# One transfer for both halves of an output store, and a new order of the same work, in a fused attention and spectral-gate kernel

## The chip, the cores and the metric

One core of a Trainium2 chip runs the whole program. The metric is the device time of one execution in microseconds; the profile is one execution taken by the hardware profiler. The engines are PE (matmul), DVE, ACT, POOL and SP; SP, POOL and ACT issue transfers, and 16 DMA engines carry them.

## The reference

Batch 8, sequence S = 3136, width D = 256, d_qk = 64, all float32:

```python
scores = (1.0 / S) * np.matmul(z, z.transpose(0, 2, 1))
x = u * np.matmul(np.maximum(scores, 0.0) ** 2, v)
proj = x @ w_proj                        # D -> 3 D
x1, x2, x3 = proj[..., :D], proj[..., D:2*D], proj[..., 2*D:]
x2_conv = irfft(rfft(x2, axis=1) * rfft(filter_fft, axis=0), axis=1)
out = (x1 * x2_conv * x3) @ w_out
```

## The kernel before

**Tiling.** The sequence is laid out as 64 x 49 (`N1`, `N2`): position n = 49 n1 + n2. A tile of 128 rows holds 64 values of n1 for two values of n2, one in rows 0 to 63 and one in rows 64 to 127. There are 25 such tiles (`NT`; the last has 64 rows), in seven chunks of columns, `CHUNKS` = 512 five times, then 256 and 320. `runs(lo, hi)` gives, for tiles lo to hi, the pieces of 64 rows: which half of the partitions (0 or 1), which tiles, and the first n2 in DRAM.

**Stages.** For each batch and chunk, PE makes scores of zT with zT (`score_mm`, two tiles at a time into a pair of PSUM banks), ACT or DVE takes the maximum with 0 into `R` (L2047, L2049) and the square into `A` (L2056, L2058; a ring of 8 buffers), and PE sums `A` against v into `ps_o` (`weigh`, `weigh_rows` by quarters of the array, L624 and L1847). Scores are symmetric: SP transposes `A` by DMA into `M1`, `M2e` or `M2o` (L1976) for the next two chunks, so an `A` buffer is free only when both the sum and the transpose have read it. `xT` (L2102) multiplies by `uT`, which SP also makes by a DMA transpose (L1647). The projections follow, then a transform along the sequence in two steps with a trip through DRAM between: `s_t` goes to `spec` (L1115), comes back as `spec_in` (L1146), is multiplied by the filter's spectrum (L1432 and on) and transformed back, `gs_t` goes to `spec` (L1480), and comes back as `conv_in` (L1175, two buffers).

**The end of a chunk (`add_end`).** PE transforms `conv_in` (`mm`), DVE multiplies by the gate into `yT` (`ev`, L1529), PE multiplies by w_out (`mo`), ACT or DVE copies to the output tile `ost` (`eo`; four tiles of 256 float32, two buffers), and `store` sends it to DRAM. Batches 0 to 5 are stored by SP; batch 6 by POOL; batch 7, the last, by POOL, ACT and SP, each piece by itself. The ends of a batch run among the next batch's attention.

**What sets the order.** A planner (`Plan`) goes through all tasks with estimated costs and emits each engine's instructions in the order in which it starts them. `ORDER` is a string with one letter for each PE task (S: scores; W and w, v: sums whole or by halves of the rows; Q: the four-quarter transforms; A, B, Z: the queues of the projections, the ends and the last ones; lower case a, b, z, x: two tasks side by side by halves), and the planner takes the first tasks of the queue that the letter names. `ENGINES` has one letter for each task that can run on ACT or DVE (a, d). A transfer has a cost on its issuing engine, a time on a shared bus (`moves`) and a delay after it (`late`). Everything that SP issues stands in one queue in this order. The tile framework adds the semaphores from the data that is read and written.

Of the kernel before, what the change touches and what calls it, by code (L numbers as in the profile page):

```python
# [33 lines left out]
LATE_OUT = 1.5  # L34
# [10 lines left out]


ORDER = (
    "ASSASSWWSSAAwwSvwSvvSwwSvvSwSvwSwSvvSBWWWWWSSSWWwwSwSwSvvSvwwvSvvSSWWAAWWWWABWBBWAAAWASSwSwwBAAvSvSw"
    "wwSSvvwvSSvSvWWBBWBWWWBAAAAWAWWSSwSWAAWAASwSwSSvvvwwwSvSvSvBWWWAWAAAWWABSwwwwSSSvvwvvwSSvwSwvSAwvSvv"
    "WAAWWWAABBWAAWAWWWSAwSwwSvSvSvSWWWWBAWAWSwSavxAAAAwSwwSwSwSvvwSvvvSvSBWAWWBWAAAWAWWSSAWAwSSwSwwSvwSv"  # L50
    "vvSwwQwSwQSvvvSvWSvQQWWWASSAWWAAAAWAWASSwwQvQwQvSwwwSSvwQvSvSvSvWWAWAWAWAAWASSwSwwSvwvSvQvwSwSwSvwvv"
    "SSvQWWWAWWAAAWAAWAQwQSwQwwQSAWAAAvvvvSSSwwwQSvSvwQSvSvWWWWAAAWWSwwwQQwQvvSQvwvQwSvQwvwSvvSSWWWWAWAAA"
    "AAAAWAAAWSwSWWQwSwSQvvSvSWAWAWWSSWAAWWAASwSwwSwwSSvvwvwvvSwSvvvSWAWBWABWAWBAWSBABWBAASwwSvSvSwSwSvSv"
    "wwSvvSwSvWAAWAWBBAWBBSSWWAAWABWBABWABwSwSwwSSvvvwSvSvwwSvvSSWAWBABAAWAAWWBAWBAWAAASwSvSwwSvvSwwSvwSv"
    "wSvwSwQvSQvvWWWWAAWBWBwSwQvSQwwwvQSvvSwSwSwwvQQvvvSvAABAAAAWBWSQSWWAABWAAWBAAWBSwQwQvSQvwSwwvSwSvQwv"
    "wvQvSSvWSSQWWWAABAAAWWWAWAAWAAwSSwQwSQvvvSSSWWWWAWSBWSwSwSwSvvwwvSwSvwvwSSvwSvvvSWWWWAAAAWAABWBSwwSv"
    "SwSwvwSvSSwvvSvSABWWBBWBAABWBWBABAAWWAAWAAAWwSSvwSvwSvSWBBBWAAABSwwSSvwSvSWWBBBBSvWWSSWWAAAAABWAAASS"
    "wwwwQvSvQvwvSSvwwQwSvvQwQvSSvWAWWBAWAWAWAABWwQwSwwSSvwvQvSwSvQvwwSvQSvvSBWAWWBWWSQQWWAAAWQwwSwSQwwSv"
    "SwvvSwSvvSvvSWAWAWWAAWBAAWAABQwwwSwSSvvvwvSQvSWAWWWSQSWWAAWSwSwwwSwwSvwSvvvvSwvwSSvvvSWBAWAAAAABAAWB"
    "AWABAWBWABSwSvwSSSwwvwSvvwSvAAABBABWBBASwvSvSSWBAWAAAWWBWBABBWBWABAAAAABSBwSwSwSvwvvSwSSwvvwSSvwwvSv"  # L60
    "vSSAAWWWWBAWAAWABABBASwwSQvBWWvSSwwSvvQwSwwSSvvQvQWWWWSWAWASwwQvQwvwSwSwSvwQSwwvvQSvvQvvSWBAWABAAWAW"
    "AWAWAQSWASwwwQQvwvSQvwwwwSvSQvvQvSvSWWWAWAAWBAWWwwSQvwvSwwSSvSvvSAWAWAWAAWAAAAWWwSSvwSSwwwSAAvSSwwwS"
    "vvvSvvvSwSvSWWABWWBAWBWABAABABSwwwSwSSvSvvSSwwwwvSvvvSSvSWBWAAAWAWWABBBABAAWAWAABAwSwSvSwwwSvwSSwvSv"
    "vwwSSvSvvvSAAWBBBWWBWWBBAWAAwSwSwSwwwSSSvvvvwwvQvSvSvwSvSAWWAAWAWAABWWAWQQwQwwSvQwwSwvwvSvQQvvSvSWAB"
    "WBBWAAWWABSSWWQSwSvwQSvwSwQvwwwvQwQvSvvvSSSWWWWAWWAAABAAWWwSQwQvwvwQwSvvSSvSWWAWWABWSQWAASwwSwwwSSAA"
    "AASvvvSwvSwvSSvvSWWWWABWWAAWABWBSwSvSwSSwwvAAWBAABAAABBBSvvSwSwwSvvSvSWAAAWBBAWAAWBWBBAWAABBWWASSwSw"
    "SvSvSwWAABWBBBSwSwSwvSSvvSvSWWWBBAWAAAWWAAAAAWAWASSwQvwSvwSwwSvvvQSwwSvvSQWWWAWSBBWABWWQwwSvvwwQvSSv"
    "wQwwwSSvvSvvQSAWAABWAAWAWWABAWSQwQvwSwSSvwwQvQvwvSQSwwwQvvSvvSWWWQSAAWAAAWABWWBAAAAWWSwQSvwSwQSvSvAB"
    "AWSWWAWABAWWSSwSwwSSvvvSwwwSvSvwvwwSvvvWWAWBWABABAAWABBBWSwSvSwASwwvSSSvvwwSvvwSwSSvvWABBAWAWAWBBABA"
    "WAWBBAABWWBSSwwwSSvSvvSWBBAAwSwSSwSvvvwSvSSWWAWWBABWWwQwSQvvSwwSwwSQvwvwSvQvwSvQvSvSWWAWWABAWWAWABSw"  # L70
    "wQSvSwwwvSSwQwvvvQSvvQQWWWBWWAWAWAwSvSwQwSwSwwSvSvvvQvwwSwSSvvvAWAAWWWBSQBWAWWBAWABWAAQwSvwSvwSQvSWZ"
    "WWWQSSWWWWBwSSvSwwSvSvWWWWWAWWWZAAAZBAZZAZBZBZBZBZZBZZZBQZBBZQQZZQZQQQBQQQQQQQBQQBZBZZZBZZZZZBZZZZZZ"
    "BZBZBZBZBBZBBBBBBBBBBBBBBBBBBBBBBB"
)

ENGINES = (
    "aaaddddaaddaaaaadaaadadaaadadaadadaaaadddaadaaaddddadadadaaadaddaadadadaaadaaaaddadaadaaaaadaaddadad"
    "aaaaadadaddaaaaddaaaaaaaaddaaaadddaddadaaaadaaaddaddaaadaaaadddadaaadadaaaddddaadaaaaadaaaaaaaddaaad"
    "dadddadaddadadadddaaddaaddadaadaaaaaadaadaadadaadaaaaaadaaadadaaaddaadaddaaaaadddadaadadaddaaaddaada"
    "adaaaaaaaaddaadadaaddaadadadaaaadaaaaadaaaaaaaaaaaadadaaaadaaaaadaadaaaaadaadaaaaddaadaaaaddaadaaaaa"  # L80
    "daadaadaadaadadadaaaadadaadadadddadddaadaadddaaaaaaaaadadaaaaaaddadaddaaadaaaddadaaaadddaadaadaaaadd"
    "dadadaaaadaddaaddadaaaaaaaaddaaaddaaaddadadaaaaadadadaadaaaadadaaddaadaaaaaaadaaaadaaadaaadaaaaaddaa"
    "aaaaaaddaaddadadadaadaaddaaaaaddaddaaaddaaaaaddaaaaddadddaddaaddaaaadaaaadadaadaddadadddaaaaaaddadaa"
    "adaddaaaaddaaaaaaaaadaddaaadaddaaaaadaadaadaaadaaaaadddaaaaaadaaaaaaadaadaadddaaaaaaaadaaaaaaaaaaada"
    "aaaaaaaaddaddaaaaaaaddadaaaaaadaaddaadaaddadaaaaaadddaadaaaddadaaadaaaadaadddaadddaaaaaaaaadaadadaaa"
    "adadaaadaddaddaaaaaaaaadaaadaadadadaaadddaaddaadaaaaaaaaadaaaadaddaaadaaadadaaaaadaadaadaaaddaaaddad"
    "aaddaaaaadaadaaddadaaaaaaaaadaaaddaaadddaaaadadadaaadddaaaddadaaadaadaddaaaadaaadaaaddadaaadddddaadd"
    "aadaddaaddadaaaaaaaadaaddadadaaaaddddddaaadadaadadaaaadaddaaaaddadaaddaaaadaadaadaaaaaaaadaaaadaaaad"
    "adaadaaaadaaaaadadaaaadddaaadaaadaaaaaadadadaaadaaadaaaaadadaaadddaaadaaaaadaadaaaaadadaaadaddaaddda"
    "dddaadaaaaaadaadaddaadaddaaaaddaaaddaaaadadaaaaaadaaddaaaaddaaaddaadaadaaaaaaaaadddaaaaaddaddaaadaaa"  # L90
    "aaadadadaaaaddadaaaaaaaadaaaaaaaddaadaaaaaaaaaaaaaaaaaaadaaaaddaaaadadadaadddadadadaaaaaddaaaaadadda"
    "adaaaaaddaddaadadaaaadaaaaaaaaaddadaadaaadddaaddaadaaaadaadaaddaaaadddaaaadaadaaaaddaddadadaaaaadada"
    "aaaaaaddadaadadaaaaaaaadadaaaaaaadaaaadadaadaddaaaadaaddaddaaaaaadaaadadaaddadadaaadddaadaaadaaaaaad"
    "aaaaaaaadaaadaaaaaaaaaadadaaaaaaaaaadaddaaaadd"
)
KINDS = {"A": "FA", "B": "FB", "Z": "FZ", "w": "W", "a": "FA", "b": "FB", "z": "FZ"}

# [397 lines left out]
def kernel(  # L495
# [12 lines left out]
    B, S, D = u.shape  # L508
# [73 lines left out]
    o_p = Pool("ost", 2, [P, 4, D], F32)  # L582
# [284 lines left out]
    for i, (t0, t1) in enumerate(zip(z_cuts, z_cuts[1:])):  # L867
        step_ = -(-(t1 - t0) // -(-(t1 - t0) // 8))
        for g0 in range(t0, t1, step_):
            nt = min(step_, t1 - g0)  # L870
# [14 lines left out]
            n = nt * dqk  # L885
# [614 lines left out]
    def add_end(b, lasts, gtasks, cs, kind="FB", src=c_p, dsts=(o_p,), late=0, behind=(), then=(), split=False, mids=(y_p,)):  # L1500
        for at, c in enumerate(cs):
# [42 lines left out]
            ob = {}  # L1544
# [43 lines left out]

            def store(i0, n, only=(0, 1), by=nc.sync, c=c, ob=ob):
                r = rows_n1(out[b])  # L1590
                for j, lo, hi, n2 in runs(T0[c] + i0, T0[c] + i0 + n):
                    if j in only:
                        by.dma_start(out=r[:, n2 : n2 + hi - lo, :], in_=ob["o"][ds(j * N1, N1), i0 : i0 + hi - lo, :])
# [602 lines left out]
```

## Time and profile before

| | us |
|---|---|
| median of 3 runs | 970.39 (969.7 to 977.35) |
| the profiled execution, its own time | 974.9 |
| its span, first to last instruction | 973.1 |

The profile shows each engine's busy time and its share of the span; the packets of each DMA queue (q1: SP's transfers, q0: POOL's, q10: ACT's) with the time that they took as a share of 16 engines; the chain of work that ended last, followed back from the last instruction; groups of equal instructions (line, engine, operation, out<-in, shape, count, then busy us and mean ns, then idle time before them and what ended it); and the transfers by line with their size. A time of landing is given for POOL's transfers alone. In 40 slices of the span the DMA engines and the bytes that they moved are:

```profile
DMA  9999899877999989997999779997999978995667
GB/s 153 172 190 150 142 178 175 175 135 174 192 211 180 148 186 209 184 151 163 198 182 189 128 141 201 201 171 134 179 175 205 214 140 171 215 194 121 190 169 233
```

The digits are tenths of the time (9 is 90% or more).

### The profile page before, as it was taken

To read this page: it belongs to the slowest core of one execution; us is meant where nothing else is said; L and a number is where in the kernel's file an instruction comes from. 1 tells how busy PE (TensorE), PEld (TensorE's weight loads), DVE (VectorE), ACT (ScalarE), POOL (GpSimd) and SP (SyncE) were. 2 spreads that over 40 slices of the span, in tenths; PEclk is the share of its full clock that TensorE was granted. 3 is DMA by queue.
4 is the path that set the end of the run, shared out by engine and by line. 5 is a ranking of instruction groups with operands and counts; after the bars stand their busy time and mean duration, and the time that the engine had idled before them with its cause. 6 is when DMAs were issued, how large, how long until landed. Compare 5 with 4: busy or idle time off the path is not lost.

```text
span 973.1 us, 26702 instructions
## 1 busy us (share of the span) xinstructions
PE 933.5 (96%) x10403; PEld 516.1 (53%) x10403; DVE 856.1 (88%) x1484; ACT 843.3 (87%) x1169; POOL 197.4 (20%) x426
## 2 busy tenths in 40 slices
PE   7999999999999999899998999998999999999895
PEld 3444555465555655465544665555555565556554
DVE  8888799989999988898887998896999999899785
ACT  7976899998799989899887999888988989998573
POOL 5222212220302211122111221222012220101031
PEclk9999999999999999999999999998999999999988
DMA  9999899877999989997999779997999978995667
GB/s 153 172 190 150 142 178 175 175 135 174 192 211 180 148 186 209 184 151 163 198 182 189 128 141 201 201 171 134 179 175 205 214 140 171 215 194 121 190 169 233
DMA packets 332430, 170.76 MB, mean 175 GB/s; under 512 B 242598, under 2 KB 307942, under 8 KB 332304
## 3 DMA queue, kind: packets, MB, share of 16 engines
q1 hardware_dynamic: 302424, 132.28, 67.7%
q0 software_dynamic: 29168, 35.13, 25.4%
q8 instruction: 81, 1.33, 0.6%
q10 hardware_dynamic: 712, 1.66, 0.6%
q14 instruction: 45, 0.37, 0.1%
HBM read 90.26 MB, written 53.35 MB: 148 GB/s over the span
## 4 chain that ended last, share of the span: by engine, by line
PE 79%; DMA 10%; DVE 4%; ACT 3%; issue 2%; SPq 2%; DVEq 0%; POOL 0%; ACTq 0%; POOLq 0%
PE ps_s L624 32%; PE ps_o_t L1847 29%; PE ps_o_t L624 17%; DMA M2e_t<-A_t 2%; DMA M_t<-A_t 1%; DMA spec<-s_t 1%; DMA M_t<-spec_in_t 1%; DMA M2o_t<-A_t 1%; ACT R_t L2047 1%; ACT A_t L2056 1%; DMA A_t<-spec 1%; DMA spec<-gs_t 1%; DVE R_t L2049 1%; DVE xT_t L2102 1%; DMA conv_in_t<-spec 1%
## 5 line engine op out<-in xcount | busy, mean ns | idle before, releaser
L2047 ACT ACTIVATE R_t<-ps_s 128x1024 f32<-128x1024 f32 (+4 forms) x347 | 322.8, 966 | 31.1 <-PE ps_s L624 22.6
L1847 PE MATMUL ps_o_t<-A_t,v_t 64*64 64x512 bf16 (+3 forms) x3852 | 319.8, 355 | 0.1
L2056 ACT ACTIVATE A_t<-R_t 128x1024 bf16<-128x1024 f32 (+2 forms) x311 | 300.9, 995 | 20.0 <-DMA M2o_t<-A_t 7.2
L1847 PEld LDWEIGHTS <-v_t 64*64 64x64 bf16 (+1 forms) x5296 | 185.5, 103 | 153.4 <-PE ps_o_t L1847 32.2
L2058 DVE TENSOR_TENSOR A_t<-R_t 128x1024 bf16<-128x1024 f32 (+4 forms) x181 | 201.1, 1126 | 20.9 <-ACT R_t L2047 11.8
L2049 DVE TENSOR_SCALAR R_t<-ps_s 128x1024 f32<-128x1024 f32 (+2 forms) x165 | 183.0, 1120 | 25.3 <-PE ps_s L624 15.1
L624 PE MATMUL ps_s<-zT_t 64*64 64x512 bf16 (+5 forms) x1558 | 185.8, 352 | 12.6 <-ACT gs_t L699 3.8
L624 PE MATMUL ps_o_t<-A_t,v_t 128*128 128x512 bf16 (+2 forms) x760 | 178.3, 354 | 0.1
L749 POOL COPY tick<-xT_t 1x1 bf16<-1x1 bf16 x54 | 10.3, 190 | 661.9 <-DVE xT_t L2102 661.9
L624 PEld LDWEIGHTS <-v_t 128*128 128x128 bf16 x1046 | 95.0, 98 | 84.8 <-issue 23.3
L624 PE MATMUL ps_s<-xT_t,wp 128*128 128x512 bf16 (+2 forms) x434 | 110.5, 353 | 0.3 <-DVE yT_t L1529 0.3
L699 ACT ACTIVATE x_t<-ps_s 128x512 bf16<-128x512 f32 (+2 forms) x155 | 84.2, 577 | 29.8 <-PE ps_s L624 25.4
L624 PEld LDWEIGHTS <-zT_t 64*64 64x64 bf16 (+1 forms) x1591 | 66.3, 102 | 73.0 <-issue 31.7
L1432 DVE TENSOR_TENSOR xh<-xh,H 128x1024 bf16<-128x1024 bf16 x120 | 81.8, 685 | 7.4 <-ACT xh L699 6.0
L2102 DVE SCALAR_TENSOR_TENSOR xT_t<-ps_o_t,uT_t 128x256 bf16<-128x256 f32 (+2 forms) x224 | 75.2, 381 | 12.1 <-issue 6.2
L1330 DVE TENSOR_TENSOR gate_t<-ps_s,x_t 128x256 bf16<-128x256 f32 (+2 forms) x216 | 72.7, 383 | 9.0 <-PE ps_s L624 5.1
L1847 PE MATMUL ps_o_t<-M_t,v_t 64*64 64x512 bf16 (+3 forms) x912 | 75.3, 363 | 0.8 <-DMA M_t<-spec_in_t 0.8
L1529 DVE TENSOR_TENSOR yT_t<-ps_s,gate_t 128x512 bf16<-128x512 f32 (+2 forms) x99 | 59.8, 621 | 11.2 <-PE ps_s L624 9.5
L740 POOL DMA_DIRECT2D un_t<-in_u_dram x112 | 60.0, 557 | 7.7 <-issue 4.0
L759 POOL DMA_DIRECT2D v_t<-in_v_dram x112 | 59.3, 551 | 6.9 <-issue 4.1
L699 ACT ACTIVATE s_t<-ps_s 128x512 bf16<-128x512 f32 (+1 forms) x86 | 50.1, 593 | 11.9 <-PE ps_s L624 11.5
L624 PEld LDWEIGHTS <-wp 128*128 128x128 bf16 x448 | 42.1, 98 | 33.6 <-issue 4.5
(177 smaller groups left out, 1030.7 us busy)
## 6 DMA issues: line engine op xcount, KB each, us to landing
out_dram<-ost_t SPq DMA_DIRECT2D x60, 256.0 KB
spec<-s_t SPq DMA_DIRECT2D x96, 128.0 KB
spec_in_t<-spec SPq DMA_DIRECT2D x56, 192.0 KB
spec<-gs_t SPq DMA_DIRECT2D x56, 192.0 KB
v_t<-in_v_dram POOLq DMA_DIRECT2D x80, 128.0 KB, 5.3
un_t<-in_u_dram POOLq DMA_DIRECT2D x80, 128.0 KB, 6.3
conv_in_t<-spec SPq DMA_DIRECT2D x34, 256.0 KB
out_dram<-ost_t SPq DMA_DIRECT2D x18, 128.0 KB
```

What stands on the lines that cost most here:

```text
L624: inst = nc.tensor.matmul(o, *args, **kw)
L699: got = nc.scalar.activation(out_, in_, AF.Copy)
L740: nc.gpsimd.dma_start(out=t[ds(j * N1, N1), lo - t0 : hi - t0, :], in_=x[:, n2 : n2 + hi - lo, :])
L1330: got = nc.vector.tensor_tensor(g[:, ::-1] if h == 0 else g, p, x, ALU.mult)
L1432: nc.vector.tensor_tensor(x[:, 1 - i], x[:, 0], h, ALU.mult)
L1529: got = nc.vector.tensor_tensor(yb["y"][:, dh, 0:w], p, gates[b, c, dh][:, 0:w], ALU.mult)
L1847: row_sums[dh] = h, nc.tensor.matmul(*args, **kw)
L2047: has_read(nc.scalar.activation(r, p, AF.Relu), p)
L2049: has_read(nc.vector.tensor_single_scalar(r, p, 0.0, ALU.max), p)
L2056: nc.scalar.activation(a, r, AF.Square)
L2058: (nc.vector if e == "DVE" else nc.gpsimd).tensor_tensor(a, r, r, ALU.mult)
L2102: nc.vector.scalar_tensor_tensor(x, f, inv_s2, ut, ALU.mult, ALU.mult)
```

## The change

`store` gets a second way. Where the two pieces of a store (rows 0 to 63 and 64 to 127) have the same tiles, one transfer is issued with both: its output side has an outermost step of two pieces, then 64 rows, then the contiguous columns; its tile side is the 128 rows. That holds for the chunks 0 to 5 of the batches 0 to 6 (36 stores on SP, 6 on POOL). The last chunk, whose last tile has 64 rows, and batch 7, whose pieces go to different queues, are stored as before. The planner's cost of such a store on SP falls from 1.3 to 0.85. Both strings are replaced; what each task computes stays.

```diff
 ORDER = (
-    "ASSASSWWSSAAwwSvwSvvSwwSvvSwSvwSwSvvSBWWWWWSSSWWwwSwSwSvvSvwwvSvvSSWWAAWWWWABWBBWAAAWASSwSwwBAAvSvSw"
+    "ASSASSSWWAAwSwSvSvwSvwwSvSwvSSvwwSvvSSWWWWWSSWBWwwSwwSvvwwSSvvSvSvSWAAWWWWWABWBBWAAWAAwSwSwwSBWASvv"
...
 ENGINES = (
-    "aaaddddaaddaaaaadaaadadaaadadaadadaaaadddaadaaaddddadadadaaadaddaadadadaaadaaaaddadaadaaaaadaaddadad"
+    "aaaddddaaddaaaddaaaaaadaaadadaadadaddddddaadaaaddddadadadaaadaddaaddadaddadaaadadaaaadaddaddaaaadaaa"
...
             def store(i0, n, only=(0, 1), by=nc.sync, c=c, ob=ob):
                 r = rows_n1(out[b])
-                for j, lo, hi, n2 in runs(T0[c] + i0, T0[c] + i0 + n):
+                got = runs(T0[c] + i0, T0[c] + i0 + n)
+                if only == (0, 1) and len(got) == 2 and got[0][1:3] == got[1][1:3]:
+                    (_, lo, hi, n2), (_, _, _, m2) = got
+                    o = r[:, n2 : n2 + hi - lo, :]
+                    o = bass.AP(o.tensor, o.offset, [[(m2 - n2) * D, 2], list(o.ap)[0], [1, (hi - lo) * D]])
+                    by.dma_start(out=o, in_=ob["o"][:, i0 : i0 + hi - lo, :].rearrange("p t d -> p (t d)"))
+                    return
+                for j, lo, hi, n2 in got:
                     if j in only:
                         by.dma_start(out=r[:, n2 : n2 + hi - lo, :], in_=ob["o"][ds(j * N1, N1), i0 : i0 + hi - lo, :])
...
-                s_ = on("SP", lambda nt=nt, store=store: store(0, nt), 1.3, [*oe, *behind], prio=1, moves=0.45 * nt, late=LATE_OUT * (dst is o_p))
+                s_ = on("SP", lambda nt=nt, store=store: store(0, nt), 0.85 if c < NC - 1 else 1.3, [*oe, *behind], prio=1, moves=0.45 * nt, late=LATE_OUT * (dst is o_p))
```

How SP's queue stands at the first store of batch 0, among the attention of batch 1: the store, then transposes of scores (`M_t`, `M2e_t`) and of u (`uT_t`); a row is a line, the transfer and the shape of its output. Before:

```order
L1175 DMA conv_in_t<-spec_0_61 128x4x256
L1115 DMA spec_1_60<-s_t 128x2x256
L1593 DMA out_dram<-ost_t 64x1024 x2
L1976 DMA_TRANSPOSE M_t<-A_t 128x8x128
L1647 DMA_TRANSPOSE uT_t<-un_t 128x8x128
L1976 DMA_TRANSPOSE M_t<-A_t 128x8x128
L1976 DMA_TRANSPOSE M2e_t<-A_t 128x8x128 x2
```

and now:

```order
L1115 DMA spec_1_60<-s_t 128x2x256
L1175 DMA conv_in_t<-spec_0_61 128x4x256
L1596 DMA out_dram<-ost_t 2x64x1024
L1983 DMA_TRANSPOSE M_t<-A_t 128x8x128
L1654 DMA_TRANSPOSE uT_t<-un_t 128x8x128
L1983 DMA_TRANSPOSE M_t<-A_t 128x8x128
L1983 DMA_TRANSPOSE M2e_t<-A_t 128x8x128 x2
```

The two stores of 64 rows have become one of 2 x 64 rows; four transposes stand behind it as before.

Later in the same batch, SP's queue from a pair of transposes on: the stores of further chunks, the load of the last end chunk (`conv_in_t`) and the first loads of batch 1's spectrum (`spec_in_t`). Before:

```order
L1976 DMA_TRANSPOSE M_t<-A_t 128x8x128 x2
L1702 DMA_TRANSPOSE zT_t<-zd_t 128x8x128
L1647 DMA_TRANSPOSE uT_t<-un_t 128x8x128
L1976 DMA_TRANSPOSE M2o_t<-A_t 128x8x128 x2
L1593 DMA out_dram<-ost_t 64x1024 x2
L1175 DMA conv_in_t<-spec_0_61 128x3x256
L1146 DMA spec_in_t<-spec_1_60 48x2048 x2
```

and now:

```order
L1654 DMA_TRANSPOSE uT_t<-un_t 128x8x128
L1983 DMA_TRANSPOSE M2o_t<-A_t 128x8x128
L1115 DMA spec_1_60<-s_t 128x2x256
L1596 DMA out_dram<-ost_t 2x64x1024 x2
L1175 DMA conv_in_t<-spec_0_61 128x3x256
L1115 DMA spec_0_59<-s_t 128x2x256
L1146 DMA spec_in_t<-spec_1_60 48x2048 x2
```

One more whole store has moved here, so that two merged stores follow each other, with the `conv_in` and spectrum loads behind them.

Near the start, DVE's queue where the first scores are squared (`A_t<-R_t`) and `xT` of chunk 0 is made. Before:

```order
L2049 TENSOR_SCALAR R_t<-ps_s_140 128x1024
L2058 TENSOR_TENSOR A_t<-R_t 128x1024 x2
L703 COPY T_220<-ps_s_139 128x128
L703 COPY T_220<-ps_s_139 128x64
L2058 TENSOR_TENSOR A_t<-R_t 128x1024
L2102 SCALAR_TENSOR_TENSOR xT_t<-ps_o_t,uT_t 128x4x64 x4
```

and now:

```order
L2056 TENSOR_SCALAR R_t<-ps_s_141 128x1024
L2065 TENSOR_TENSOR A_t<-R_t 128x1024 x3
L2109 SCALAR_TENSOR_TENSOR xT_t<-ps_o_t,uT_t 128x4x64 x4
L2065 TENSOR_TENSOR A_t<-R_t 128x1024
L703 COPY T_220<-ps_s_139 128x128
L703 COPY T_220<-ps_s_139 128x64
```

The copies of the transform's table have gone behind `xT`, and a square has moved ahead of it. Over the whole program the order moves nine of the 128x1024 squares from ACT (247 to 238) to DVE (141 to 150) and adds 158 rows on PE (20,806 to 20,964), where more sums run by quarters.

More of the change, by code (lines that the diff above doesn't have):

```diff
@@ L47 @@
 ORDER = (
-    "ASSASSWWSSAAwwSvwSvvSwwSvvSwSvwSwSvvSBWWWWWSSSWWwwSwSwSvvSvwwvSvvSSWWAAWWWWABWBBWAAAWASSwSwwBAAvSvSw"
[L49 to L72, printed above, removed]
@@ L73 @@
-    "BZBZBZBZBBZBBBBBBBBBBBBBBBBBBBBBBB"
+    "ASSASSSWWAAwSwSvSvwSvwwSvSwvSSvwwSvvSSWWWWWSSWBWwwSwwSvvwwSSvvSvSvSWAAWWWWWABWBBAWAAWAAwSwSwwSBWASvv"
+    "SwSwSSvvvSvSWWWWBBWWBAAWABWWAAwSSSwWAAAWBAvSwSvwwwSSvSvSvvSAWWWBWAAAWWwSSwSWAWAvwvSwSwSvwvvwSSvSvWWA"
+    "WAWAABBAWWWWWAwSSwwSvSvSvSAAWWWWBAAWWSwSavxSwBAAAwSwSvvwSvwSwSvSvvWBWAWAAWAAWWASSAWAWWSSSwwwSvSvQwwS"
+    "wQwvSSvvwSvvQvWQSWAAWWSSAAWWAAAWWASwwQvQvQSwwwSQvSvSwvSvwSSvWWWAWAAWAAAWSSSwwwwSvQvSwSwvSvwSvwvvSSvQ"
+    "WWWAWWAWAAAWAAQQwSwwQwSQvWAAAAvvvSSwSvwwQwSQvSvvSSAWWWWAAWWQwwSvQvQwwQSvwQvwSvQvwwSSvvSWWAAAWWWAAAAA"
@@ new lines @@
+    "WAAAWwSSWWQSSwwQvvvSSWAAAWWWSSSWAAWAWAwSwwSSwwSvvvvwSwwSvSvvwvSvAWBWAWBAWWABBWAABBSwwSvSwvSSvwSvwSwS"
+    "vvSwSvWAWAABBBWASSAWABWWBABWBWAWwSwSwSwSvvSwvwvSwvSSvSvWAWABWAAAWBBBWAABAAAAAWWSwSwSSwwSvvwwSvvSwSvS"
+    "vwvSvwQvQWWBWWABAWWSwSwQwQvwQwSvwvSSvvwQvwQwSvSvvBAAAABWWSQSWWAABWBWAAAAWAABSwQvQSwwwSwwSQSvwwvvQSvQ"
+    "vSvvSWWWWSQAWAAWAWAWBAWAAAASwSQwwQSvvSvSSWWWWAWSSBWWSSwwSvvwwSwSSvvwwwvSSvvSvWWWAAWAWAAABWBwSwSwSwwS"
+    "vvvSSvwSvSvSWWBBABABWBWAAABBWAWBWAAABAWBWASwSwSvvwSABABSwwvSvwwvSSvwSvSBBWBBWSSvSWBBAWAAWAWAAAAAWSSw"
@@ new lines @@
+    "wQSwwSvQvvSwvwwwQSwQvvvSQvvSWAWAAWAWWBAWWwSwQwSwwQSvvvSSQvwQwwvSvSvSvBWAWABWWQQSWWABWAAwwwQSSwwwQSvv"
+    "vSwvwSSvvSvvSWBWWWAAAAWAAAWSwQvwwSSvwSvwQvvSWWWWQSSWWAAAWAwwSwSSwwwwSvSvvSvvwvvSvwSSvWWAWWBAABAAAABA"
+    "WABAABWABASwSwSSwSvwwwvvSSvwSvvBAAABBvSwwSBBWBASvvSAWBWBAWABBABBWAAWAABAAABWSwSwwASvvSSwwSvSwvwwSvSS"
+    "vvvSWWWWBAWAABAWABBAwQSwBAWWSSSvwwwwvQwSSvvSvvvQQSWWWSWAWAWQwwSvwQwvwSSQvwwSSvvwwQvSvvQSvWWABBWWAAWA"
+    "AWAAwQwQwAWASvQwSvvSQwwvwSQvSvvQwSSvWWWWABWAWAAwSwwQSvwwwvvSvSvvSSWWAAAWAAWAWAAAWwSSvSwSwwwSAASSvwwS"
@@ new lines @@
+    "wvvwSvSSvvvvSWAWWBWBWABWABAABABwSSwwwSSSvwvSvSwwwvSvvSSvvSWWABAAWBBAABAWWAAWBABAAAWwSwSSvwwwSSvSvSvw"
+    "vwwwSSvvvvSSWBAWABBBWBWWBAAAAAWSwSwwwSSvvSvwSvwSwwwQvvSvvSvSWAAWWWAABAWAWWQQwQwwSQvwwSwwQvvSvSvQvvSW"
+    "BAWABAWWWBBSSWWSQwSvwwSwQSvwQwvSwwQvQvvvvSwSSvWWWBWAAWAAAAWWSQwwQvwwQwvSvvSSvSWAWAWAWAWBWSwSSwSwwwQv"
+    "SAAAASwwSvSvwvvvSvSvSWWBWWAAAWABABWWASSwSvwSSwvwwBBBWAABBASvvSvwwSvSwvSSvSWBWWBAABBWAWAABAABAAAAWWSS"
+    "wSvwwSSvWAABABBWABBSSvwSSwwSvSvvSWWABBWWAWAAAWAAWAAASwwwSQvSvwvSwSwwwSQvvSvvSvWWQSWWAWABWWBWBAQwSvww"
@@ new lines @@
+    "SQvwvwQSwSQvvvSwSSvWAAWWABWAABWAAWSQwSvwQvwwSQSvwvwQvSwwvQwSQvvvSSWWWWQSAWAWwAAAABWAWBAAAQvwSwSwSvSQ"
+    "vSvSAWAWBWWAWABAWwSSvwSwwwvSSvSwwwvwvSSSvvvvWWWBABAWAAWABABWSwwSSvWBBAAwSwSSvvvSwSvwSwSvvSWBBWWBBWWA"
+    "BWBAAABAABABWAWSSwwwSSSvvwvSBBAAwwSvSSvvSwSSvWWWWBAWSAWBWSQwwwSvSwwvvQSvvQwwQSvwvSwSSvvQWWAAWWAABWWA"
+    "BWwSwSQvwSvwwQSwvSvvwQQvvQSWWWWWAAWBAWwSwQvSvSwSwSvvwwSQvvwwSwSSvvvWABWBAWWAWQSWAWAWAWZBAAQwSwSwQvSS"
+    "vvBWWWBWQSSWWwwSSvwvSwwSvvvSWAWWWWWWWAZZAZAZAZAZBBBZZBBZZBZZZBQZBZZQQZBQQBQQQQQQQZQQBQQBZZZBZZBZZZZZ"
@@ L74 @@
+    "ZZZZZBZBBZBZBZBBZBBBBBBBBBBBBBBBBBBBBBBB"
 )
 ENGINES = (
-    "aaaddddaaddaaaaadaaadadaaadadaadadaaaadddaadaaaddddadadadaaadaddaadadadaaadaaaaddadaadaaaaadaaddadad"
[L78 to L91, printed above, removed]
@@ L92 @@
-    "adaaaaaddaddaadadaaaadaaaaaaaaaddadaadaaadddaaddaadaaaadaadaaddaaaadddaaaadaadaaaaddaddadadaaaaadada"
-    "aaaaaaddadaadadaaaaaaaadadaaaaaaadaaaadadaadaddaaaadaaddaddaaaaaadaaadadaaddadadaaadddaadaaadaaaaaad"
-    "aaaaaaaadaaadaaaaaaaaaadadaaaaaaaaaadaddaaaadd"
+    "aaaddddaaddaaaddaaaaaadaaadadaadadaddddddaadaaaddddadadadaaadaddaaddadaddadaaadadaaaadaddaddaaaadaaa"
+    "adaaadadaddaaaaaddaadaaaaddaadaaddaaaadadddaaadaadaddaadadadadaaddaadaddadaadaadaaddaaaaadadaadaadad"
+    "dadaaddadaddadadddaaddaaddadaadaaaadadaadaaadadaaadaadadaaadadaaaddaadaddaaaaaddaadaaaadaddaaaadddaa"
@@ new lines @@
+    "adaaaaaaaaadaadadaaddaadadadaaaaadaaaaddadaaaaaaaaadadddaadaaaaadaadaaaaadaaaadaaddaaaaaaaddadaaaaaa"
+    "dddadaadddadaaaaadddadadaaaddadddadddaddaaaddaaaaaaaaadadaaaaaadaaaaddaaadaadadadaaaadddaadaaaadddad"
+    "daaaadadaaaddaaaaddaaaaaadaaadaaddaaaddadadaaadaaadadaaaaaaadadaaadaadaaaaaaaddaaadaaadaaadadddaddaa"
+    "aadaaadaaaddadaddaaaaaaddaadaaaaaaaaaddaaadadaddaaaadaaaaaddadaaaddadaaaaaaaadadddadadadaaaaaaddadaa"
+    "adaadaadddaddaaadaaaddddadaaaddaaaadaaadaadaaadaaaaadddaddadaaaaaaaaaaaaadaaddadaaaaadaaaaadaaaaaada"
@@ new lines @@
+    "aaaaaadaddaddaadaadaddaaaaddaaaaaaddaadaddddadddaadaaaadadaddaaddaaaadaddaddddaadaaddadadaaaaadadaaa"
+    "adadaaadaddaddaaaaadadaadaaaaaaddadadaaddaaadadaaaadaaddadaaaaaadadaaaaaadadaaaaadaadaadaaaaaaaaddad"
+    "aadaaadaadaadaaaaadaaaaaaaadaddadaaadadaddaddadadaaadddaaadaddddadaadadadaaadaaadaaaddddaaaadaadaaaa"
+    "aaaaddaaddadaaaaaaaadaaddadadaaaaadaaadaddaddaadadaaaddadddadaaaadadaaaaaaaddaadaaaaaadaaddaaaaaaaad"
+    "adaaadadaaaaaaadadaaaadddaaaaadaaaaaaaadaaadaaaaaaaaaaddadadaaadddaaaddaadadaadaadaadadaaadaddaaddda"
@@ L95 @@
+    "dddaadadddaadaaadaaaadaddadaaddaaaddaadadadaddaadaaadaaadaadaaadadadaadadaaadaaadddaaadaadaddaaadaaa"
+    "aaadadadaaaadaaddaaaaadadaaaaaaaddaadaaaaaaaaaaaaaaaaaaadadaaadaaaaadaaaaaddadaaadaaaaaaddaaaaaaddad"
+    "aadaaddaaaaadadadaaaadaadaaddaaaadaaaadaaadaaddaddaaaadddaaadadaaaadddaaaadaadaaaaaaaddadaddaaaadada"
+    "aaaaaadaaddaaaaddaddaaadadaaaaaaddaaaadadaadadaaaaaaaaddadaadaaaadaaadadaaddadadaadddaaaaaaaaaaaaaad"
+    "aaaaaaaadaaadaaaaaaaaaadadaaaaaaaaaadadaddaadd"
 )
```

## The prediction

> **What bounds the kernel now.** I read the page first (busy time, chain of waits, DMA queues and issues), then the DMA view and the busy time by stretch of the window in which one batch is stored, then the long chain and the waits for the transfers in it. The page:
>
> ```profile
> span 973.1 us, 26702 instructions
> PE 933.5 (96%) x10403; PEld 516.1 (53%) x10403; DVE 856.1 (88%) x1484; ACT 843.3 (87%) x1169; POOL 197.4 (20%) x426
> q1 hardware_dynamic: 302424, 132.28, 67.7%
> q0 software_dynamic: 29168, 35.13, 25.4%
> PE 79%; DMA 10%; DVE 4%; ACT 3%; issue 2%; SPq 2%; DVEq 0%; POOL 0%; ACTq 0%; POOLq 0%
> ```
>
> PE is busy in 96% of the span and makes 79% of the chain that ends last. But the packets of the two large queues (SP's transfers on q1, POOL's on q0) fill 67.7 + 25.4 = 93% of the 16 DMA engines' time, and the chain runs through DMA for 10%, some 97 us. So this kernel has two resources near their end, and the second one is what the change touches. The span of the profiled execution is 973.1 us and its own time 974.9; the median of the shown runs is 970.4, so I make the sum as a difference to 974.9 and set it on 970.4.
>
> Where DMA stands in the chain (start, length, transfer):
>
> ```profile
> 399.90 7.64 DMA spec<-s_t
> 503.60 8.47 DMA M_t<-A_t
> 515.24 9.10 DMA M2e_t<-A_t
> 648.31 10.46 DMA M2o_t<-A_t
> ```
>
> and SP's own line of time around the second of them (start, time in the queue, line):
>
> ```profile
> 497.92 2.10 SPq L1593 DMA_DIRECT2D out_dram<-ost_t  x2
> 500.29 3.22 SPq L1976 DMA_TRANSPOSE M2e_t<-A_t  x1
> 503.60 6.68 SPq L1976 DMA_TRANSPOSE M_t<-A_t  x2
> ```
>
> A transpose of scores that SP issues soon after a pair of stores lands 8.5 us after its issue and something waits for its end. There is no slack to speak of behind a store, even today. The waits say the same: squares stand still until a transpose has given their A buffer back.
>
> ```profile
> ACT A_t L2056 <- DMA M2o_t<-A_t: 7.2, 3, 5.4
> ACT A_t L2056 <- DMA M2e_t<-A_t: 6.0, 2, 5.0
> DVE A_t L2058 <- DMA M2e_t<-A_t: 5.4, 2, 3.5
> ```
>
> **The change, part by part.**
>
> *Fewer issues.* On SP 36 pairs of stores become 36 single ones (30 of 512 KB, 6 of 256 KB), on POOL 6 pairs do (5 and 1).
>
> ```profile
> out_dram<-ost_t SPq DMA_DIRECT2D x60, 256.0 KB
> out_dram<-ost_t SPq DMA_DIRECT2D x18, 128.0 KB
> 350.65 1.69 SPq L1593 DMA_DIRECT2D out_dram<-ost_t  x2
> 354.41 1.28 SPq L1593 DMA_DIRECT2D out_dram<-ost_t  x2
> 364.86 1.18 SPq L1593 DMA_DIRECT2D out_dram<-ost_t  x2
> 378.25 1.16 SPq L1593 DMA_DIRECT2D out_dram<-ost_t  x2
> 398.59 1.21 SPq L1593 DMA_DIRECT2D out_dram<-ost_t  x2
> 417.62 1.18 SPq L1593 DMA_DIRECT2D out_dram<-ost_t  x2
> ```
>
> (The 18 of 128 KB are 12 of the pairs' halves and 6 of the last tile rows, which stay apart.) A pair takes about 1.18 us of SP's queue, so one issue less is 0.59 us, 36 x 0.59 = 21 us of SP in all. SP's queue is 2% of the chain, so I give this 0, and at most 2% of 21, under 1 us.
>
> *The new strings.* The same arithmetic in another order. On DVE nine squares of 128x1024 more, on ACT nine less, and some more evictions go the same way:
>
> ```profile
> L2056 ACT ACTIVATE A_t<-R_t 128x1024 bf16<-128x1024 f32 x247 | 257.8, 1067 | 16.5 <-DMA M2o_t<-A_t 7.2 <-DMA M2e_t<-A_t 6.0 <-DVE R_t L2049 1.6
> L2058 DVE TENSOR_TENSOR A_t<-R_t 128x1024 bf16<-128x1024 f32 x141 | 169.9, 1219 | 16.0 <-ACT R_t L2047 7.2 <-DMA M2e_t<-A_t 5.4 <-ACT s_t L699 2.2
> ```
>
> That is 9 x 1.07 = 10 us off ACT and 9 x 1.22 = 11 us onto DVE, both of which stay under PE's 933.5. PE's 158 added rows are the same sums cut into quarters. What an order can win is PE's idle time, 973.1 - 933.5 = 39.6 us, of which the first and the last microseconds stay; what it can lose has the same size. I take -3 us, with -10 and +10 as ends.
>
> *The shape of the transfer.* This is the term that decides. Before, each piece is 64 rows of 4 KB, out and in. Now the output side is counted as 2 pieces, 64 rows, 4 KB, outermost first, and the tile's side as 128 rows, 1, 4 KB. On how many of the 16 engines does that lie? The trace shows how transfers are divided. In the last 12 us ACT's queue (q10) carries five stores of 64 rows and nothing else; in the 19 us from 921 it carries four loads of nine rows and nothing else:
>
> ```profile
> gs_t<-spec ACTq DMA_DIRECT2D x4, 36.0 KB
> q10 hardware_dynamic: 400, 1.11, 28.8%
> q10 hardware_dynamic: 72, 0.15, 3.7%
> ```
>
> (window 962 to 974, then 921 to 940; packets, MB, share of 16 engines). 400 packets are 5 x 64 rows and 80 more, 16 for each store. 72 are 4 x 9 rows and 36 more, 9 for each load. So a transfer ends with one small packet on each engine that took part: 16 with 64 rows, 9 with 9. It is divided by its outermost count. No transfer in this trace has different outermost counts on its two sides. With 2 on one side and 128 on the other I take 2: every row shown is divided by whole steps of the outer count, and two steps give two engines.
>
> The Trainium skill says so outright: by its page "DMA: Bandwidth & Descriptors", section "Why a DMA increments its semaphore by 16 and not by 1", the number of engines is the largest up to 16 that divides the slowest count of both sides, and they are the lowest-numbered ones; for 2 and 128 that is 2. The trace agrees for 64 and for 9 rows, and cannot show 2 against 128.
>
> Price of a store on two engines. The same row of q10 gives a row's time: 28.8% of 16 engines x 12 us = 55.3 us for 1.11 MB, so 0.20 us for 4 KB and 0.10 us for 2 KB. Today a pair puts 8 rows on each engine, 1.6 us (0.8 us for 2 KB rows). On two engines it puts 64 rows on each, 13.0 us (6.5 us): 11.4 us more on those two (5.7 us), and nothing on the other 14. Everything SP issues behind it has a sixteenth of its bytes on these two and ends when that part ends.
>
> What of it reaches the end? Take one batch's stores, all six between 350 and 430 (rows above). The stretch (length, busy PE, PEld, DVE, ACT, POOL, clock, DMA share, GB/s):
>
> ```profile
> 350.00:430.00 80.00, 76.69 (x869) 41.07 (x868) 71.42 (x124) 69.61 (x94) 15.24 (x32) 1.00 1.07 186
> ```
>
> - Upper end: the share is true occupation. The two engines carry 1.07 x 80 = 85.6 us now, less today's stores 5 x 1.6 + 0.8 = 8.8, plus the new 5 x 13.0 + 6.5 = 71.5: 148 us of work in 80 us, 68 us too much. Over the whole span the share is 93%, so next to nothing is worked off in the rest of the batch: +68 us a batch.
> - Lower end: a share above one shows that packets overlap on an engine, so it overstates the need. The most that the trace shows is the 436 GB/s in this row (GB/s in 40 slices of 955 to 972), 27 GB/s an engine, 4 KB in 0.15 us.
>
> ```profile
> GB/s 153 181 318 252 370 354 365 380 383 436 387 390 366 270 135 87 29 0 0 260 193 164 241 328 222 301 297 183 241 193 183 366 260 318 376 390 285 236 72 0
> ```
>
> By bytes the stretch needs 186/436 x 80 = 34 us, less 6.6 of today's stores, plus 5 x 9.6 + 4.8 = 52.8: 80 us in 80. Then nothing is left over: +0 a batch.
>
> Between 0 and 68 I take the middle, 34 us: the small packets of the transposes do not run at the peak rate, and the chain's rows of 8 to 10 us behind stores show that lateness is paid at once; but PE's waiting thins the other traffic out, which works against the upper end. SP stores six batches (batches 0 to 5): 6 x 34 = 204 us, ends 0 and 408. Behind such a store SP's queue holds the transposes, uT, the conv_in loads of the next end chunk and the spec loads (the order rows above), and for these wait, in turn, the squares (A buffers), PE's mirrored sums, DVE's xT, and PE's end chunks. The A ring's eight buffers and the two of conv_in and ost cover part of 11.4 us; when that cover is gone the rest is PE's.
>
> *POOL's six stores.* These rows carry the price now (last number: us to landing):
>
> ```profile
> out_dram<-ost_t POOLq DMA_DIRECT2D x8, 256.0 KB, 3.4
> out_dram<-v_t POOLq DMA_DIRECT2D x2, 256.0 KB, 4.6
> ```
>
> They have few followers, in the last batch. On 16 engines they cost 0; on two, at most one more batch's 34 us. I take 0 and keep 34 for the range.
>
> Sum: 974.9 + 0 - 3 + 204 + 0 = 1175.9 for an execution like the profiled one; on the median, 970.4 + 201 = 1171. I say 1175.
>
> **Rivals.**
>
> *Sixteen engines after all* (the other side): the transfer is divided by its 128 rows of the tile. Then each engine has the same 8 rows, 1.6 us, and only the 21 us of SP and the new order are left: 970.4 - 3 = 967, between 958 and 985. For it: the tile's side is as good a count as the other, and the trace does not show which one rules. Against it: the count of end packets follows the outermost step. It decides from the point where the split gives 16 parts; below that the rows per engine rise. The same skill page, in "Rules for kernel authors", speaks for the change: two transfers to disjoint partition halves share the same engines anyway, use one of 128 partitions. Here that would give these 967; but the rule below it, on using all 16 engines, wants the large count outermost, and this transfer has 2 there.
>
> *Two engines, but absorbed*: the rings of A, M and conv_in take the lateness, and only one store a batch is paid in full, 6 x 11.4 = 68 us: 970.4 + 68 = 1038, from 985 to 1060. For it: the lower end above. Against it: the waits for A buffers today.
>
> *The two engines become the bound throughout*: the share is true occupation, 970.4 + 408 - 3 = 1375, from 1320 on. For it: a DMA share of 1.07 in the stretch. Against it: a share over one cannot be occupation.
>
> **How the numbers follow.** Forecast (two engines, half of the excess paid, 1060 to 1320) 0.67; sixteen engines 0.15; absorbed 0.10; bound throughout 0.08. Two engines in any form are 0.85. The range reaches from 990 to 1340: it holds the forecast (0.67), nearly all of the absorbed case (0.09) and the lower half of the last (0.04), 0.80 together; the sixteen-engine case lies outside. One per cent (9.7 us; the three runs before spread by 0.8%) is about what a measurement of this kernel can tell from no change. Slower by more: 0.85 and the slow tail of the sixteen-engine case (worse strings), 0.03, together 0.88. Within: 0.08 of that case. Faster by more: its remaining 0.04.
>
> **What would show it.** Two engines: SP's queue q1 loses 36 x (160 - 130) = 1080 packets (a pair has 128 rows and 32 end packets, the merged store 128 and 2); sixteen: 36 x 16 = 576. The DMA share of a stretch of stores falls well under one while transposes behind a store take over 12 us in the chain, and DMA's part of the chain rises from 10% to 20% or more. ACT and DVE wait longer for A buffers, PE idles some 200 us more, nearly all of it before 845, in the batches that SP stores. The forecast is wrong if q1 loses about 576, or if it loses 1080 and the chain still has DMA at about 10%.

## The result, and the profile after

| | before | changed |
|---|---|---|
| median, us | 973.87 (969.7 to 991.12, 4 runs) | 1217.9 (1216.08 to 1228.77, 4 runs) |
| ratio, 95% interval | | 1.2547 [1.2432, 1.2662] |
| profiled execution, own time / span, us | 974.9 / 973.1 | 1216.08 / 1214.3 |

The change costs a quarter of the time. The ratios here and below leave out executions more than 1.5% above the fastest of the same kernel (here 991.12), so a ratio can differ a little from that of the medians. The page of the changed kernel (busy times; the queues' packets, MB and share of 16 engines; the chain by engine; the stores):

```profile
span 1214.3 us, 26789 instructions
PE 994.4 (82%) x10482; PEld 541.8 (45%) x10482; DVE 873.2 (72%) x1505; ACT 839.7 (69%) x1148; POOL 194.9 (16%) x420
q1 hardware_dynamic: 301344, 132.27, 65.0%
q0 software_dynamic: 34000, 35.15, 20.0%
PE 51%; DMA 31%; DVE 5%; ACT 4%; issue 4%; SPq 3%; another core or an unknown queue 0%; ACTq 0%; DVEq 0%
out_dram<-ost_t SPq DMA_DIRECT2D x30, 512.0 KB
out_dram<-ost_t POOLq DMA_DIRECT2D x4, 512.0 KB, 18.6
```

Three things are to be read. SP's queue carries as many bytes as before (132.28 and 132.27 MB) in 302424 - 301344 = 1080 packets fewer, which is 36 x 30 to the packet: each merged store ends on 2 engines (2 end packets in place of 32). DMA's part of the chain rises from 10% to 31%. And no engine has become busier by much (PE the most, from 933.5 to 994.4 us, of which more at the end); PE goes from 96% to 82% of a longer span.

The two engines can be seen at work. The DMA view of the changed kernel from 400 to 412 us, in 40 slices (share in tenths of 16 engines, then GB/s):

```profile
DMA  9768997798998532111101111186211110111110
GB/s 191 120 150 178 198 203 155 126 154 135 176 154 161 130 82 68 48 34 41 36 19 32 22 32 29 26 251 169 60 43 44 63 55 41 55 55 55 55 55 41
```

From the middle on the share is one tenth, with a burst between, and at the end 55 GB/s in slice after slice: two engines of 16 are an eighth of the share, and 55 / 2 = 27.5 GB/s each is 4 KB in 0.149 us. From 409.2 to 413 us SP's queue is alone, and its packets take 13.0% of 16 engines, 2.1 engines:

```profile
q1 hardware_dynamic: 70, 0.20, 13.0%
```

The other 14 stand idle while a 512 KB store runs out. SP's line of time there (start, time in the queue, line):

```profile
396.52 5.90 SPq L1596 DMA_DIRECT2D out_dram<-ost_t  x1
402.52 4.77 SPq L1115 DMA_DIRECT2D spec<-s_t  x1
...
413.47 0.52 SPq L1596 DMA_DIRECT2D out_dram<-ost_t  x1
414.09 3.29 SPq L1115 DMA_DIRECT2D spec<-s_t  x1
417.48 10.13 SPq L1983 DMA_TRANSPOSE M_t<-A_t  x1
```

Even the issue is held back: a transpose that takes 1.2 to 1.3 us of SP's queue where nothing holds it, and took 3.2 to 3.3 us behind a pair of stores in the prediction's rows, takes 10.13 us behind the merged store. In the chain (start, length) this transpose and others now stand with 11.7 to 16.7 us, beside stores and a load that a later step waits for:

```profile
236.56 12.11 DMA M_t<-A_t
391.82 14.67 DMA out_dram<-ost_t
417.48 16.66 DMA M_t<-A_t
479.10 11.70 DMA M_t<-A_t
559.32 15.99 DMA out_dram<-ost_t
744.21 14.96 DMA spec_in_t<-spec
```

Who pays (waiting engine, what for, us in total, times, longest):

```profile
ACT A_t L2063 <- DMA M_t<-A_t: 59.7, 14, 13.4
DVE A_t L2065 <- DMA M_t<-A_t: 42.6, 6, 13.2
ACT ost_t L699 <- DMA out_dram<-ost_t: 39.4, 6, 8.8
```

The squares wait for `A` buffers, 102 us in these two rows, and evictions wait for `ost` tiles. By the Trainium skill (page "DMA: Bandwidth & Descriptors", section "Why a DMA increments its semaphore by 16 and not by 1") such a transfer lies on 2 engines; the trace agrees, with 1080 packets fewer and 55 GB/s.

### The profile page after: what moved, and what is told of

Same layout as the page of the kernel before. It is cut to its first block, busy times and chain, and to the rows that moved or that the text cites. A ratio compares the mean times of both kernels' runs of the same rounds, so it can differ in the third digit from the quotient of the medians.

```text
span 1214.3 us, 26789 instructions
## 1 busy us (share of the span) xinstructions
PE 994.4 (82%) x10482; PEld 541.8 (45%) x10482; DVE 873.2 (72%) x1505; ACT 839.7 (69%) x1148; POOL 194.9 (16%) x420
## 3 DMA queue, kind: packets, MB, share of 16 engines
q1 hardware_dynamic: 301344, 132.27, 65.0%
## 4 chain that ended last, share of the span: by engine, by line
PE 51%; DMA 31%; DVE 5%; ACT 4%; issue 4%; SPq 3%; another core or an unknown queue 0%; ACTq 0%; DVEq 0%
PE ps_o_t L1854 21%; PE ps_s L624 20%; DMA M_t<-A_t 11%; PE ps_o_t L624 10%; DMA out_dram<-ost_t 6%; DMA spec_in_t<-spec 3%; DMA conv_in_t<-spec 2%; DMA M2e_t<-A_t 2%; DMA A_t<-spec 2%; DMA spec<-M2o_t 1%; DVE R_t L2056 1%; DMA spec<-s_t 1%; ACT R_t L2054 1%; DVE A_t L2065 1%; DMA M_t<-spec_in_t 1%
## 5 line engine op out<-in xcount | busy, mean ns | idle before, releaser
L2054 ACT ACTIVATE R_t<-ps_s 128x1024 f32<-128x1024 f32 (+3 forms) x349 | 325.3, 964 | 76.4 <-PE ps_s L624 34.4
L1854 PE MATMUL ps_o_t<-A_t,v_t 64*64 64x512 bf16 (+4 forms) x3886 | 337.8, 369 | 14.6 <-issue 9.8
L1854 PEld LDWEIGHTS <-v_t 64*64 64x64 bf16 (+1 forms) x5390 | 201.2, 107 | 188.1 <-issue 45.2
L2065 DVE TENSOR_TENSOR A_t<-R_t 128x1024 bf16<-128x1024 f32 (+3 forms) x191 | 211.7, 1126 | 96.5 <-DMA M_t<-A_t 42.6
L624 PE MATMUL ps_s<-zT_t 64*64 64x512 bf16 (+5 forms) x1570 | 196.7, 366 | 54.7 <-ACT ost_t L699 24.0
L2056 DVE TENSOR_SCALAR R_t<-ps_s 128x1024 f32<-128x1024 f32 (+4 forms) x163 | 180.0, 1118 | 58.8 <-PE ps_s L624 39.3
L2109 DVE SCALAR_TENSOR_TENSOR xT_t<-ps_o_t,uT_t 128x256 bf16<-128x256 f32 (+2 forms) x224 | 75.3, 383 | 23.3 <-PE ps_o_t L624 12.1
L624 PE MATMUL ps_s<-wo,yT_t 128*128 128x256 bf16 (+1 forms) x344 | 56.7, 289 | 16.3 <-DVE R_t L2056 10.7
L699 ACT ACTIVATE ost_t<-ps_s 128x512 f32<-128x512 f32 (+1 forms) x57 | 33.4, 590 | 52.0 <-DMA out_dram<-ost_t 39.4
L699 ACT ACTIVATE xh<-ps_s 128x512 bf16<-128x512 f32 (+1 forms) x71 | 41.5, 611 | 33.4 <-PE ps_s L624 33.1
L624 PE MATMUL ps_s<-wp,xT_t 128*128 128x256 bf16 (+1 forms) x408 | 61.4, 278 | 3.3 <-ACT ost_t L699 2.5
```

The costliest lines, as they stand in the source:

```text
L624: inst = nc.tensor.matmul(o, *args, **kw)
L699: got = nc.scalar.activation(out_, in_, AF.Copy)
L1854: row_sums[dh] = h, nc.tensor.matmul(*args, **kw)
L2054: has_read(nc.scalar.activation(r, p, AF.Relu), p)
L2056: has_read(nc.vector.tensor_single_scalar(r, p, 0.0, ALU.max), p)
L2065: (nc.vector if e == "DVE" else nc.gpsimd).tensor_tensor(a, r, r, ALU.mult)
```

## The experiments

The theory is "two engines": the count of outermost steps on the output side sets how many engines a store lies on, and its rows there delay all the rest. Its rivals: "strings" (the new order costs), "one transfer" (the length of a merged store costs, wherever it lies), the shape by itself, and the place in SP's queue. Ratios are to the kernel before on the same chip.

**The new order without the merged stores.**

```diff
-                if only == (0, 1) and len(got) == 2 and got[0][1:3] == got[1][1:3]:
+                if False and len(got) == 2 and got[0][1:3] == got[1][1:3]:
```

> The changed kernel with every store again as two transfers of 64 rows; the new strings and the planner's cost stay, so PE, DVE and ACT stand in the changed kernel's order. Theory 'two engines' (a store whose output side has 2 outermost steps lies on 2 of the 16 DMA engines, and all that SP issues behind it waits there): the loss is gone, 960 to 985 us, q1 at 302424 packets again, DMA about 10% of the chain. Theory 'strings' (the new order of the tasks costs the time): 1190 to 1230 us.

Measured: 968.22 us against 978.23, ratio 0.9914 [0.9872, 0.9955], q1 302424. The loss is gone, with DMA at 11% of the chain; the order by itself gains 0.9%, and this kernel beats both others. Its busy times and its chain:

```profile
PE 927.8 (96%) x10403; PEld 520.2 (54%) x10482; DVE 867.1 (90%) x1505; ACT 834.0 (86%) x1148; POOL 196.4 (20%) x426
PE 75%; DMA 11%; DVE 6%; ACT 3%; issue 3%; SPq 1%; ACTq 0%; DVEq 0%
```

**The merged stores in the old order.** The kernel before with the new `store` and nothing else of the diff.

> The kernel before, with its own strings and costs, and the merged store on SP and POOL. 'Two engines': nearly all of the loss, 1180 to 1240 us, q1 at 301344 packets (1080 fewer). 'Strings': 965 to 985 us. If strings and stores each had a share, the two kernels of this comparison would both lie between.

Measured: 1.266 [1.2588, 1.2732], 1236.11 us, q1 301344. The whole loss, and a little more, is the stores'.

**Only SP's, and only POOL's.** The same kernel with one more condition in `store`:

```diff
-                if only == (0, 1) and len(got) == 2 and got[0][1:3] == got[1][1:3]:
+                if by is nc.sync and only == (0, 1) and len(got) == 2 and got[0][1:3] == got[1][1:3]:
```

(`nc.gpsimd` for POOL's.)

> The kernel before with SP's 36 stores merged and POOL's as they were: the main term by itself. With POOL's stores at 1.024 and all merged at 1.266, additive costs give 1.24, some 1205 to 1220 us; if POOL's and SP's stores hinder each other, less than 1.23.

> The kernel before, with only POOL's six stores of batch 6 merged. The prediction took 0 for them, at most 34 us. 'Two engines' on POOL's queue as well: landing of the 512 KB stores some 13 us or more in place of 3.4, time 970 to 1005 us; if POOL's transfers lie on 16 engines whatever their shape: landing of 4 to 6 us, 968 to 978 us.

Measured: SP's alone 1.2502 [1.2383, 1.2621], 1215.7 us against 972.03; POOL's alone 1.0243 [1.019, 1.0297]. Together 25.0 + 2.4 = 27.4%, with 26.6% measured: they add up within their intervals. POOL's stores, with POOL's alone merged:

```profile
q0 software_dynamic: 34000, 35.15, 24.7%
out_dram<-ost_t POOLq DMA_DIRECT2D x4, 512.0 KB, 16.0
out_dram<-v_t POOLq DMA_DIRECT2D x1, 512.0 KB, 23.9
out_dram<-v_t POOLq DMA_DIRECT2D x1, 256.0 KB, 21.1
```

Landing takes 16 to 24 us where 256 KB took 3.4 to 4.6. The end packets cannot tell the engines here, because this queue's count rises (see the end), but its share can. In this kernel's trace POOL's queue is alone from 943.5 to 945.9 us, behind the first merged store, and again from 949 to 952, with four issued:

```profile
q0 software_dynamic: 53, 0.07, 12.0%
q0 software_dynamic: 77, 0.24, 36.3%
```

12.0% of 16 engines is 1.9, and 36.3% is 5.8. That fits two engines for each store here too, other ones for the next store, and three stores at work in the second window. And they do have followers. The chain of this kernel in the last batch:

```profile
957.74 13.39 DMA spec<-M2o_t
971.61 14.22 DMA A_t<-spec
```

The last batch's writes of its spectrum, which POOL and SP issue behind these stores, and the loads of the end chunks take 13.4 and 14.2 us there. That they wait for the engines of these stores is read from the order and the times. In the same places of its chain the kernel before had:

```profile
944.09 3.16 DMA spec<-uT_t
951.33 7.66 DMA A_t<-spec
```

That is 27.6 us in place of 10.8.

**The count of outermost steps by itself.** The kernel before, with SP's stores as 72 transfers of 64 rows, each written as g steps of 64 / g rows; the rows are taken in strides so that the steps stay apart, and they land in another order in the output. The two lines of the edit that make the shape, with g for the number in them:

```diff
+                            row = list(o.ap)[0][0]
+                            o = bass.AP(o.tensor, o.offset, [[row, g], [g * row, N1 // g], [1, (hi - lo) * D]])
```

> The kernel before; each of SP's 72 stores of 64 rows stays a transfer of its own, but its output side is counted as 2 steps of 32 rows (every second row), so the rows inside a piece of 64 land in another order in the output. 'Two engines': as slow as the merged store, 1180 to 1260 us, q1 at 302424 - 72 x 14 = 301416 packets. Theory 'one transfer' (it costs that both halves go in one long transfer, on however many engines): 965 to 985 us, since each half is again by itself.

> As pairs_outer2, with 4 outermost steps of 16 rows in each of SP's 72 stores (the rows inside a piece land in another order). 'Two engines' in its general form (as many engines as outermost steps): 16 rows of 4 KB on each of four engines for each piece, so half the excess on each loaded engine: 24 rows a pair more than on sixteen in place of 56; between 1020 and 1110 us, q1 at 302424 - 72 x 12 = 301560 packets. If only the shape's being three steps costs (longer work in making the transfer), as slow as with 2: 1250 to 1270 us.

> As pairs_outer2, with 8 outermost steps of 8 rows. General 'engines as outermost steps': 8 rows of 4 KB a pair more on each of eight engines, 970 to 1000 us, q1 at 302424 - 72 x 8 = 301848. Shape alone: 1250 to 1270 us.

> As pairs_outer2, with 16 outermost steps of 4 rows: the control. The form of the transfer is the same three-step one, but it lies on all 16 engines: 965 to 985 us, q1 at 302424. Shape alone: 1250 to 1270 us.

The last column divides the loss by the rows of 4 KB that a loaded engine has more than before (a 256 KB pair counts as half): 33 x (128 / g - 8).

| g | q1 packets | ratio, 95% | loss, us | rows more | us a row |
|---|---|---|---|---|---|
| 2 | 301416 | 1.2949 [1.2856, 1.3042] | 288 | 1848 | 0.156 |
| 4 | 301560 | 1.1136 [1.0952, 1.1319] | 111 | 792 | 0.140 |
| 8 | 301848 | 1.0352 [1.0198, 1.0506] | 34 | 264 | 0.130 |
| 16 | 302424 | 0.9967 [0.9895, 1.0038] | none | 0 | |

All four packet counts are as expected. The time follows the number of engines and goes to nothing at 16, so neither "one transfer" nor the shape stands: these are again 72 transfers, of the same three-step form in all four. The expected times for 2 engines (1180 to 1260) and 8 (970 to 1000) were a little low, by 3 and 11 us.

The page of g = 8, where each loaded engine has only 8 rows a pair more, shows that there is no slack even for that: DMA is at 16% of the chain.

```profile
PE 70%; DMA 16%; DVE 5%; ACT 4%; issue 2%; SPq 2%; ACTq 0%; DVEq 0%
```

**By another queue.** The merged stores of SP issued by ACT.

```diff
-                    by.dma_start(out=o, in_=ob["o"][:, i0 : i0 + hi - lo, :].rearrange("p t d -> p (t d)"))
+                    (nc.scalar if by is nc.sync else by).dma_start(out=o, in_=ob["o"][:, i0 : i0 + hi - lo, :].rearrange("p t d -> p (t d)"))
```

> The kernel before, SP's 36 stores merged and issued by ACT's queue in place of SP's, at the same place of the program; POOL's stores as before. If what costs is the order in the queue (SP's transposes and loads stand behind 64 rows on two engines of their own queue): 1000 to 1110 us, since another queue's rows share those engines by turns. If it is the two engines' time (64 rows of 4 KB on each, whoever issues them): 1180 to 1250 us. q1 at 302424 - 5760 = 296664 packets either way, ACT's queue at 712 + 36 x 130 = 5392.

Measured: 1.242 [1.2256, 1.2584], 1212.61 us, with the packets moved as expected:

```profile
q1 hardware_dynamic: 296664, 114.97, 72.6%
q10 hardware_dynamic: 5392, 18.96, 4.2%
```

The place in SP's queue is not what costs: out of it the loss is the same within the intervals, and an issue takes ACT's queue only 0.52 to 1.12 us. It is the two engines' time, whoever issues.

**Half of the stores.** Merged for chunks 0, 2 and 4 alone.

```diff
-                if by is nc.sync and only == (0, 1) and len(got) == 2 and got[0][1:3] == got[1][1:3]:
+                if by is nc.sync and c in (0, 2, 4) and only == (0, 1) and len(got) == 2 and got[0][1:3] == got[1][1:3]:
```

> As sp_merged_alone, but only the stores of chunks 0, 2 and 4 are merged: 18 stores of 512 KB of 30 (and none of the six of 256 KB). If each merged store's excess on its two engines enters in full, 18 / 33 of the loss (a store of 256 KB counts as half): 0.55 x 235 = 128 us, 1090 to 1120 us. If the buffers cover a part that is exceeded only when stores follow each other closely, less: 1000 to 1070 us.

Measured: 1.1338 [1.1212, 1.1465], 1105.26 us. 13.4 of 25.0% is 0.53 of the loss for 18 / 33 = 0.55 of the rows: the loss grows in step with the stores, and the buffers cover no more of it when the stores stand further apart. It is 130 us for 18 x 56 = 1008 rows, 0.129 us a row.

No run has a third `ost` tile, so what the wait for tiles is worth by itself stays open.

## Why the prediction was right

**Mechanism.** Right at the step that decided: from the end packets of ACT's queue (16 for 64 rows, 9 for 9) the prediction took the division by outermost steps, so 2 engines for the merged store, and gave 1080 packets as the sign. It is 1080. That the side with 2 steps rules, and not the one with 128, no trace before could show; it was a choice, put down as one, and the runs with g steps against 64 rows bear it out. The rival with 16 engines, 967 us, falls; its price was nearly that of the new order alone, 968.22. The absorbed rival, 985 to 1060, falls with the measured time.

**The main term** was 204 us, 34 a batch; SP's stores alone measured 0.2502 x 972.03 = 243 us, 40 a batch. Two parts of it were off and cancelled in part, and that the sum came this near is luck to that extent. A row of 4 KB was priced at 0.20 us from ACT's stores at the end of the program, where many transfers run together; on two engines alone it is 0.149 us (55 GB/s above), the figure that the prediction had used for its lower end. And the middle between its ends, about half of the excess, was too little: at 0.149 us the excess is 1848 x 0.149 = 275 us, and 243, or 88%, reaches the end. The case in which the two engines are the bound throughout was, then, nearer to what happens than its 0.08 said; its time of 1375 was too long mostly because of the price of a row. At 0.149 us its sum for a stretch is 85.6 - 6.6 + 52.8 - 80 = 52 us, and so some 1279. That lateness behind a store "is paid at once" was right, and more sharply than the sum used it.

**The strings**: -3 us taken, within -10 to +10; measured 0.86% of 978.23, -8 us.

**POOL's stores**: 0 taken, 34 kept as the end; measured 2.43%, 24 us. This step failed in its reason: "they have few followers". The rows of POOL's own queue show the followers, the spectrum of the last batch, and nothing comes after it that could take up the time.

**Fewer issues**: 0 taken, and no run shows this term by itself: the kernel with g = 16 has the 72 issues of before.

The terms as measured, 243 + 24 - 8 = 259, against 244 between the medians.

**Signs that were forecast.** DMA at 20% or more of the chain: 31%. Transposes of over 12 us behind stores: 12.1 to 16.7. The share of the DMA engines in a stretch of stores under one: the changed kernel's 360 to 480 us against the same window before the change (length, busy PE, PEld, DVE, ACT, POOL, clock, DMA share, GB/s):

```profile
360.00:480.00 120.00, 93.90 (x993) 51.24 (x991) 80.29 (x131) 79.71 (x109) 16.43 (x35) 0.88 0.89 134
```

```profile
360.00:480.00 120.00, 116.46 (x1326) 66.21 (x1323) 105.80 (x182) 109.42 (x154) 23.39 (x49) 1.00 1.02 176
```

It fell from 1.02 to 0.89: the direction was right, "well under one" was not. PE idle "some 200 us more": 1214.3 - 994.4 = 220 us against 40, so 180. Most of it lies in the batches that SP stores: 176 us in the first 1080 us, in which all but one of SP's merged stores are issued, against 23 in the first 840 us before.

## What to carry to other kernels

Before two transfers are joined, look at the outermost count of each side of the new one: here that count, not the bytes or the number of rows, set how many of the 16 DMA engines carried it, and 2 in place of 16 cost 25%. Count packets in the profile: on SP's and ACT's queues rows plus end packets gave the number of engines of a transfer without any timing (not on POOL's). Where DMA engines are near full, as in this kernel, the price of unevenness was the time of the added rows on the most loaded engine, nearly in full (0.13 to 0.16 us for 4 KB), and neither another issuing queue nor buffers took it away.

## What had not been expected

**The clock.** The granted clock fell with PE's waiting: 0.988 before, 0.904 in the changed kernel, 0.88 in the window above where PE is busy 94 of 120 us. PE is busy 994.4 us for work that took 927.8 us in the kernel with the same order and unmerged stores. The second figure lacks 79 matmuls that its trace did not record (10403 of 10482); at its mean of 89 ns they are 7 us. So some 60 of the 246 us between the two spans are slower matmuls and 186 are idle time. How much of the 60 would have been idle time at full clock is open. The Trainium skill has this on its page "TensorE: Matmul & The Clock Gate", section "Why this matters for your kernels", as gaps of more than some 3 us between bursts of matmuls lowering the clock; the trace agrees in kind, and no run here tries the length of a gap.

**POOL's packets.** Six merged stores raised POOL's queue from 29168 to 34000 packets in each kernel that had them, 4832 more, where the count of end packets alone would have lowered it. All of them are small: with POOL's stores alone merged, the packets under 512 B of all queues go from 242598 to 247430, which is these 4832. Nothing here tells what they do.

**Two engines twice.** With 2 steps, 72 separate stores cost more than 36 merged ones with the same rows on the same number of engines, 1.2949 against 1.2502. The reason is open.
